# A retention, channel-mixing and gating kernel: the last two token blocks of the first channel mixing as a pair with seven products

## The chip, the cores and the metric

The kernel runs on one core of a Trainium2 chip. The metric is device time in microseconds (us) of one execution; several runs are taken and their median is given. The profile and the trace come from one further execution, whose own time is given beside its span.

Engines are named as in the profile: PE is TensorE's matmul, PEld its weight load, DVE is VectorE, ACT is ScalarE, POOL is GpSimd, SP is SyncE, which issues nearly all DMAs of this kernel in one queue.

## The reference

The reference computes three layers one after the other on 8 sequences of 576 tokens with 512 channels. The change lies in the second, in the first of its two channel products (`w_ch1`, 512 x 2048), and moves work of the second one (`w_ch2`).

```python
scores = scale * np.matmul(q, k.transpose(0, 1, 3, 2))      # retention, 8 heads of 64
attn = np.matmul(scores * Dmat, v)                          # Dmat: gamma ** (i - j), causal
xt = x.transpose(0, 2, 1)                                   # x: attn, heads joined
u = x + (xt @ U @ V).transpose(0, 2, 1)                     # low-rank token mixing, rank 32
ch = np.maximum(u @ w_ch1, 0.0) @ w_ch2                     # 512 -> 2048 -> 512
x = u + ch
k = np.maximum(xk @ w_k, 0.0)                               # xk, xr: x mixed with its neighbour
out = 1 / (1 + np.exp(-(xr @ w_r))) * ((k * k) @ w_v)
```

## The kernel before

The 4608 tokens are nine blocks of 512, numbered 0 to 8. A product in full precision is made of three matmuls: each operand is split into an upper part (a cast, on ACT) and a remainder (a subtraction, mostly on DVE), and upper x upper, lower x upper and upper x lower are summed in PSUM. All matmuls of the large products are 128x128 weights against 512 columns.

The order of all instructions is written out by hand: each engine runs its instructions in the order in which the code issues them, and SP's DMAs stand in one such order too. Tiles come from pools of slots (`big`, 35 slots of 4 KB a partition; `big2`, 16; `small`, 9 of 2 KB); a tile waits until its slot's last reader is done.

There are four stages.

1. **Retention** with the low-rank mixing, and beside it the first channel product. A step (`step_of`, L1307) does 128 tokens of one sequence; five steps make a sequence of 58 us. After the small matmuls of a step, `hidden` (L1058) issues some units of the first channel product out of the list `ready`. One unit (`hidden_part`, L360, three parts) gives 128 hidden features of one token block: 12 matmuls (L368), a relu on ACT (L374), a store to DRAM. 144 units in all: 9 blocks x 16 feature groups. `FULL` says how many follow each step of a sequence: 3, 3, 4, 4, 2. `todo` holds the mixing products of a finished sequence (`mix`, L1027), and at its end `mix_store` (L1033), which splits the mixed tokens into both blocks that the sequence touches, stores them, and puts 16 units in `ready`.
   When `todo` is empty, `slot` (L173) advances other jobs by a stage: they turn 64-bit weights into float32, split them and park them in DRAM (`park` L215 for `w_v`; `block_weight` L251 for `w_k` and `w_r`, with the four sums of blocks that a seven-product scheme needs).
2. **The rest of the first channel product**: when retention ends, 35 units are left (three of block 6 and the 32 of blocks 7 and 8), which run alone on PE. Beside them `second_weight` (L391) turns the eight groups of `w_ch2` into split block sums in SBUF; the last of them (`late`) works on DVE.
3. **The second channel product**, blocks 0 to 7 as four pairs with seven products instead of eight (`products`, L518): each item loads 1 MB of stored hidden values (`load_item` L464, four items ahead), forms sums (`sums_item` L476, two ahead, DVE), splits them (`split_item` L487, one ahead, ACT and DVE), and runs 24 or 18 matmuls (L540) into eight PSUM banks. Block 8 follows alone (`project`, L620 to L622).
4. **Gates, keys and values** of the third layer, the first two with seven products as well (`product`, L1411; its operands come from the generator `operands`, L679).

The pool of PSUM banks is handed over between stages 2 and 3 (`first_psum.close()`).

Of the kernel before, what the change touches and what calls it, by code (L numbers as in the profile page):

```python
# [30 lines left out]
L = 64  # L31
# [5 lines left out]
NF = DF1 // 128  # L37


@with_exitstack  # L40
def retention_mixer_kernel(ctx: ExitStack, tc: tile.TileContext, io):
# [142 lines left out]
    class Weight:  # L184
# [66 lines left out]
    def block_weight(g, pool, src, kept, kind):  # L251
        raw, a, got = [], [], {}

        def load():
            for i in range(2):
                r = pool.tile([128, 512], I64, tag="unit", name=f"w{kind}raw{g}_{i}")
                c0 = (g + len(kept) * i) * 128
                nc.sync.dma_start(
                    r.rearrange("p (k n) -> p k n", n=128),
                    src[:, c0:c0 + 128].rearrange("(k p) n -> p k n", p=128),  # L260
                )
                raw.append(r)
# [12 lines left out]
        def sums():  # L275
            x = got["s"] = [
                cv.tile([128, 512], F32, tag="cf", name="cf", bufs=5).rearrange(
                    "p (s n) -> p s n", n=256
                )
                for i in range(2)  # L280
            ]
            f = got["f"]
            a11, a12, a21, a22 = f[:, 0, :256], f[:, 0, 256:], f[:, 1, :256], f[:, 1, 256:]
            s1, s3, s2, s4 = (x[i // 2][:, i % 2] for i in range(4))
            nc.gpsimd.tensor_tensor(s1, a21, a22, op=ALU.add)
            nc.gpsimd.tensor_tensor(s2, s1, a11, op=ALU.subtract)
            nc.gpsimd.tensor_tensor(s3, a11, a21, op=ALU.subtract)
            nc.gpsimd.tensor_tensor(s4, a12, s2, op=ALU.subtract)

        def parts(i):  # L290
            h, l = (
                pool.tile([128, 4, 256], F32R, tag="unit", name=f"w{kind}{x}{g}_{i}") for x in "hl"
            )
            for w in range(2):
                if i == 0:
                    src = got["f"][:, w].rearrange("p (s n) -> p s n", n=256)
                else:
                    src = got["s"][w]
# [15 lines left out]
        ]  # L314

# [75 lines left out]
    def second_weight(j, pool):  # L391
        raw, got = [], {}
        out = pool if j else big2

        late = j == NF // 2 - 1

# [7 lines left out]
        def down():  # L404
            got["a"] = unit(big if late else big2, F32, f"w2a{j}")
            got["f"] = unit(big if late else big2, F32, f"w2f{j}")
            for i in range(2):
                high(got["a"][:, i], raw[i])
                low(got["f"][:, i].bitcast(U32), raw[i])
# [5 lines left out]
        def sums():  # L415
# [4 lines left out]
            eng = nc.vector if late else nc.gpsimd  # L420
# [24 lines left out]
        def parts_of_one(i):  # L445
            for lo in range(2):
                part(i, lo, nc.vector)

        return [
            load, *[None] * (5 if late else 1 if j else 2), down, lambda: fill(0), lambda: fill(1), sums,  # L450
            *(
                (lambda: parts_of_one(0), lambda: parts_of_one(1)) if late
                else (lambda: parts(0, nc.vector), lambda: parts(1, nc.gpsimd))
            ),
        ]
# [223 lines left out]
    def operands(x, q, a, b, nm):  # L679
        def upper(n, src):  # L680
            h, l = (unit(big, F32R, f"{nm}{y}{n}_{q}")[:, :, :columns(q)] for y in "hl")
# [8 lines left out]
        t = unit(big, F32, f"{nm}t_{q}")[:, :, :columns(q)]  # L690
# [5 lines left out]
        less(b[0], b[0], a[0])  # L696
        yield
        lower()
        lower = upper("t1", b[0])
        yield  # L700
        less(t, b[1], b[0])
# [49 lines left out]
    with ExitStack() as st:  # L751
# [280 lines left out]

        def mix_store(b):  # L1033
# [11 lines left out]
        todo, ready = [], []  # L1045

# [5 lines left out]
        def later(b):  # L1052
            for k in range(KD):
                for s in range(2):
                    todo.append(lambda k=k, s=s: mix(b, k, s))
            todo.append(lambda: mix_store(b))
# [110 lines left out]
        for at in (9, 10, 11, 13, 15, 17, 19):  # L1167
            waiting.insert(at, [None])
        for at, job in zip((0,4,8,12,16,20), jobs):
            waiting.insert(at, job)  # L1170

# [118 lines left out]
        FIRST, FULL = (2, 1, 2, 1, 1, 2, 2, 3), (3, 3, 4, 4, 2)  # L1290
# [15 lines left out]

        def step_of(i):  # L1307
# [8 lines left out]
            if p == NC - 1:  # L1316
                plan(i + 2, low_rank_sum, b)
                plan(i + 3, later, b)
            for fn, args in due.pop(i, []):
                fn(*args)  # L1320
            if not ready:
                mixes(9)
            n = FIRST[i - NC] if i < len(FIRST) + NC else FULL[p]
            for x in range(2):
                hidden((n + 1 - x) // 2, False)
                stages(2 * i + x)
                if i > 2 * NC + 2 and not todo:
                    quiet.append(i)
                    slot(new=len(quiet) % 2 == 1)
# [4 lines left out]
        for i in sorted(due):  # L1334
            for fn, args in due.pop(i):
                fn(*args)
            hidden(2)
        while todo:
            hidden(1) if ready else mixes(1)
        while waiting or going:  # L1340
            slot()

# [6 lines left out]
    for j in range(NF // 2):  # L1349
        waiting.append(second_weight(j, big))  # L1350
    ticks = []

    def tick():
        ticks.append(0)
        slot(new=len(ticks) in (27, 4 * (len(ticks) // 4) + 1) and len(ticks) < 28)

    while len(ready) > 2 * NF:
        hidden(1, False)
        tick()
    ready.sort(key=lambda x: x[1] + 2 * (x[0] == NB - 1))  # L1360
    while ready:
        if len(ready) in (7, 5, 3, 1):
            load_item(3 - len(ready) // 2)
        if len(ready) in (3, 1):
            sums_item(len(ready) == 1)
        if len(ready) == 2:
            split_item(0)
        hidden(1, False)
        tick()
    first_psum.close()  # L1370
    psum.append(ctx.enter_context(tc.tile_pool(name="psb", bufs=1, space=PSUM, reuse_waits="tile")))
    for n, (q, h, j) in enumerate(ITEMS):
# [4 lines left out]
        if n + 1 < len(ITEMS):  # L1377
# [5 lines left out]
        if n == len(ITEMS) - 1:  # L1383
            split_hidden(0)
        products(n)
# [286 lines left out]
```

## Time and profile before

| | us |
|---|---|
| median of 3 runs | 1353.21 (1351.12 to 1356.03) |
| the profiled execution's own time | 1349.82 |
| its span, first to last instruction | 1348.0 |
| PE busy, of the span | 1332.4 (99%) |
| DVE, ACT, POOL busy | 845.5, 652.1, 337.4 |
| TensorE's mean granted clock | 0.995 |
| moved by DMA | 308 MB, 229 GB/s |

A busy PE is a modelled time: matmuls overlap, and one of 512 columns is shown as up to 0.39 us long while the next starts sooner. What one costs in a row of them is read from the chain of work that ended last, where pieces of the same line are merged with their count. An idle time in brackets stands ahead of an instruction, with what ended it.

### The profile page before, as it was taken

The numbers are of one execution on the slowest core, as the hardware profiler recorded it, in microseconds if no ns is written. First come the engines' busy times: TensorE is split into PE (matmuls) and PEld (weight loads), VectorE is DVE, ScalarE is ACT, GpSimd is POOL, SyncE is SP. The second block draws the span as 40 slices with busy tenths as digits, with TensorE's granted clock in tenths as the row PEclk, the third lists the DMA queues.
The fourth block names the chain that finished last, engine by engine and source line by source line (L and its number), as shares of the span: only waits on it lengthen the run. The fifth ranks groups of instructions, "written<-read, shape, count | busy, mean of one in ns | idle before, by whom it ended". The sixth has DMA issues, their size and how long they took to land.

```text
span 1348.0 us, 25775 instructions
## 1 busy us (share of the span) xinstructions
PE 1332.4 (99%) x10263; PEld 1096.0 (81%) x10263; DVE 845.5 (63%) x1173; ACT 652.1 (48%) x1133; POOL 337.4 (25%) x284
## 2 busy tenths in 40 slices
PE   7999999999999999999999999999999999999998
PEld 4778888888887888888888888888888888888897
DVE  4763333243340223989897987897787787787753
ACT  4664444434343466544444434565464464464431
POOL 2121232412222154023222112204204204204212
PEclk8899999999999999999999999999999999999999
DMA  8977698776653657969697886794174174273372
GB/s 292 333 260 247 210 334 286 273 275 242 215 209 149 211 198 256 318 234 313 196 308 274 296 277 223 261 334 185 65 272 163 70 271 160 71 273 124 111 282 77
DMA packets 124377, 308.26 MB, mean 229 GB/s; under 512 B 14496, under 2 KB 27040, under 8 KB 124256
## 3 DMA queue, kind: packets, MB, share of 16 engines
q1 hardware_dynamic: 124256, 306.60, 65.5%
q8 instruction: 81, 1.33, 0.4%
q14 instruction: 40, 0.33, 0.1%
HBM read 215.33 MB, written 91.23 MB: 227 GB/s over the span
## 4 chain that ended last, share of the span: by engine, by line
PE 93%; DVE 4%; DMA 1%; issue 1%; ACT 1%; SPq 0%; POOL 0%; DVEq 0%; ACTq 0%
PE h L368 29%; PE v L1507 14%; PE ga L540 6%; PE gc L540 6%; PE gd L540 5%; PE kc L1411 4%; PE kd L1411 4%; PE ka L1411 4%; PE gb L540 3%; PE kb L1411 2%; PE rd L1411 2%; PE rc L1411 2%; PE ra L1411 2%; PE xn L962 2%; PE up L854 1%; PE dn L876 1%
## 5 line engine op out<-in xcount | busy, mean ns | idle before, releaser
L374 ACT ACTIVATE hs<-h 128x512 f32<-128x512 f32 x144 | 86.0, 598 | 211.8 <-PE h L368 208.2
L1463 POOL TENSOR_TENSOR vl<-m,vh 128x512 fp32r<-128x512 f32 (+1 forms) x40 | 47.6, 1191 | 310.3 <-ACT vh L1462 240.0
L834 DVE TENSOR_TENSOR pm<-up,dtab 128x512 f32<-128x512 f32 (+1 forms) x40 | 25.4, 636 | 134.1 <-PE up L820 121.6
L499 ACT CAST sbh<-rb 128x1024 fp32r<-128x1024 f32 x64 | 67.3, 1052 | 59.9 <-PE gd L540 43.4
L500 DVE TENSOR_TENSOR sbl<-rb,sbh 128x1024 fp32r<-128x1024 f32 x64 | 85.3, 1333 | 7.8 <-ACT sbh L499 7.7
L1507 PE MATMUL v<-vh,wv_0u 128*128 128x512 f32 x288 | 88.8, 389 | 0.0
L1507 PE MATMUL v<-vh,wv_1u 128*128 128x512 f32 x288 | 88.7, 389 | 0.0
L500 DVE TENSOR_TENSOR sal<-ra,sah 128x1024 fp32r<-128x1024 f32 (+1 forms) x64 | 65.5, 1023 | 20.6 <-PE gd L540 12.7
L499 ACT CAST sah<-ra 128x1024 fp32r<-128x1024 f32 (+1 forms) x64 | 53.6, 837 | 50.7 <-DVE ra L481 19.6
L782 POOL TENSOR_TENSOR kv<-kv,ktab 128x512 f32<-128x512 f32 (+1 forms) x40 | 39.8, 995 | 142.7 <-DMA kv<-in_kv 101.0
L1463 POOL TENSOR_TENSOR vl<-c,vh 128x512 fp32r<-128x512 f32 (+1 forms) x40 | 62.2, 1574 | 25.8 <-ACT vh L1462 25.8
L1507 PEld LDWEIGHTS v<-vh,wv_1u 128*128 128x128 f32 x288 | 54.1, 188 | 11.2
L1507 PEld LDWEIGHTS v<-vh,wv_0u 128*128 128x128 f32 x288 | 53.9, 188 | 11.0
L1462 ACT CAST vh<-m 128x512 fp32r<-128x512 f32 (+1 forms) x40 | 23.2, 579 | 75.7 <-DVE m L1461 75.7
L1031 DVE TENSOR_TENSOR xt<-mx,xt 128x256 f32<-128x256 f32 x64 | 28.8, 457 | 49.2 <-PE mx L1027 49.0
L1507 PE MATMUL v<-vl,wv_0u 128*128 128x512 f32 x144 | 56.0, 389 | 0.0
L1507 PE MATMUL v<-vl,wv_1u 128*128 128x512 f32 x144 | 56.0, 389 | 0.0
L653 ACT ACTIVATE tp<-x2l,omu 128x511 f32<-128x511 f32 x72 | 50.9, 712 | 2.7 <-DMA x2l<-xb 1.4
L584 POOL TENSOR_TENSOR x<-x,ur 128x512 f32<-128x512 f32 x16 | 24.3, 1530 | 107.5 <-DMA ur<-ub 53.5
L557 POOL TENSOR_TENSOR m<-m,ur 128x512 f32<-128x512 f32 x8 | 12.2, 1557 | 133.6 <-ACT m L554 133.6
L1461 DVE SCALAR_TENSOR_TENSOR m<-m 128x512 f32<-128x512 f32 (+1 forms) x40 | 44.8, 1120 | 1.4
L1411 PE MATMUL kc<-kht,wk 128*128 128x512 f32 (+1 forms) x160 | 45.5, 368 | 0.0
(290 smaller groups left out, 3740.3 us busy)
## 6 DMA issues: line engine op xcount, KB each, us to landing
wk<-keys SPq DMA_DIRECT2D x80, 512.0 KB, 6.0
hp<-hs SPq DMA_DIRECT2D x128, 256.0 KB, 2.9
rb<-hp SPq DMA_DIRECT2D x64, 512.0 KB, 5.8
wr<-gates SPq DMA_DIRECT2D x40, 512.0 KB, 6.9
qk<-in_qk SPq DMA_DIRECT2D x32, 512.0 KB, 5.6
kv<-in_kv SPq DMA_DIRECT2D x32, 512.0 KB, 6.2
ra<-hp SPq DMA_DIRECT2D x32, 512.0 KB, 7.1
ur<-ub SPq DMA_DIRECT2D x18, 512.0 KB, 5.8
```

The costliest lines, as they stand in the source:

```text
L368: nc.tensor.matmul(hps[t, f], w.part(lo, k, fo), u[k // 2][:, k % 2, :], start=(part == 0 and k == 0), stop=(part == 2 and k == KD - 1),)
L374: nc.scalar.activation(h, hps.pop((t, f)), AF.Relu)
L499: nc.scalar.copy(hi_, src)
L500: nc.vector.tensor_tensor(lo_, src, hi_.bitcast(F32), op=ALU.subtract)
L540: nc.tensor.matmul(group[g][p], l[:, col(p)], r, start=(h == 0 and j == 0 and i == 0), stop=(i == 2 and last), skip_group_check=True,)
L653: nc.scalar.activation(tp[:, 1:], x[:, :BT - 1], AF.Copy, scale=omu[:, j, k:k + 1])
L782: nc.gpsimd.tensor_tensor(k, k, ktab[:, p, :n].to_broadcast([128, n, NP, D]), op=ALU.mult)
L1031: nc.vector.tensor_tensor(u, ps[:, :n], u, op=ALU.add)
L1411: nc.tensor.matmul(ps[b], l, r[:, i], start=(part == 0 and i == 0 and j == 0), stop=(i == 1 and j == 2), skip_group_check=True,)
L1461: nc.vector.scalar_tensor_tensor(x, x, 0.0, x, op0=ALU.max, op1=ALU.mult)
L1463: eng.tensor_tensor(l, x, h.bitcast(F32), op=ALU.subtract)
L1507: nc.tensor.matmul(vacc[t][o], w.part(lo, g, col(o)), x[:, i, :], start=(g == 0 and i == 0 and j == 0), stop=(g == NG - 1 and i == 1 and j ...
```

## The change

Blocks 7 and 8 are taken out of the list of units and computed as a pair after retention, in eight groups (`first_group`) of seven products with six matmuls each. Their operands are seven sums and splits of the two blocks (`operands`, now with a pool argument, and writing into its first block instead of its second). The weights' sums are formed on DVE during retention out of the split weights (`first_sums`, one step in each `beside`), stored in DRAM, and loaded and split again a group ahead. The relu of these blocks works in SBUF, after the sums.

Four of the eight groups of `w_ch2` (`KEPT` = 4 to 7) are converted during retention by `block_weight` with a new argument `by_row`, parked, and loaded in the third stage (`load_second`); the other four are converted beside the new groups. The raw loads of `w_v` are issued two slots ahead of their conversion instead of one. Jobs begin in three of eight slots instead of every second. In sequences 2 to 6 the first part of a block is no longer split by the sequence before, but loaded again (`fetch_head`) and split (`split_head`) with its own sequence. The last sequence has 2, 2, 3, 3, 3 units after its steps. Cut to its core:

```diff
+HF = NF // 2
+PAIR = (NB - 2, NB - 1)
+KEPT = 4
-                waiting.append(convert(fetch, parts, 128, 512, store))
+                job = convert(fetch, parts, 128, 512, store)
+                waiting.append([job[0], None, *job[1:]])
+    def first_sums(g):      # stages: whole(0), whole(1), sums(0), sums(1), store
+        def whole(i):       # twice: 128x512 = upper part + remainder, on DVE
+            f = g + HF * i
+            for k in range(2):
+                nc.vector.tensor_tensor(
+                    got["x"][:, 2 * i + k].rearrange("p (k n) -> p k n", n=128),
+                    w.h[k][:, :, c].bitcast(F32), w.l[k][:, :, c].bitcast(F32), op=ALU.add)
+        def sums(i):        # two of 128x256 each
...
+    def load_first(g):
+        fraw[g] = (big if g < 2 else big2).tile([128, 4, 256], F32, tag="unit", name=f"fr{g}")
+        nc.sync.dma_start(fraw[g], kept_1[g])
+
+    def split_first(g):
+        x = fraw.pop(g)
+        fs[g] = h, l = tuple(
+            (big2 if g else big).tile([128, 4, 256], F32R, tag="unit", name=f"f{y}{g}") for y in "hl")
+        nc.scalar.copy(h, x)
+        nc.vector.tensor_tensor(l, x, h.bitcast(F32), op=ALU.subtract)
+    def load_second(j, i):  # two loads of 512 KB
...
-            load, *[None] * (5 if late else 1 if j else 2), down, lambda: fill(0), ...
+            load, None, lambda: words(0), lambda: words(1), lambda: fill(0), lambda: fill(1), sums,
+            lambda: parts(0, nc.vector), lambda: parts(1, nc.gpsimd),
         def mix_store(b):
-            split_u(b, BT - o, u[:, :, :o], o)
-            split_u(b + 1, 0, u[:, :, o:], S - o)
+            if b < PAIR[0]:
+                split_u(b, BT - o, u[:, :, :o], o)
+            if b == 0:
+                split_u(1, 0, u[:, :, o:], S - o)
-            ready.extend((b, f) for f in range(NF))
-            if b == B - 1:
-                ready.extend((b + 1, f) for f in range(NF))
+            if b < PAIR[0]:
+                ready.extend((b, f) for f in range(NF))
...
+        def beside():
+            quiet.append(0)
+            slot(new=len(quiet) % 8 in (1, 4, 6))
+            if sums and len(quiet) > 8:
+                sums.pop(0)()
+            n = ... FULL[p] if b < B - 1 else LAST[p]          # LAST: 2, 2, 3, 3, 3
...
+        gen = operands(x1, 0, even, odd, "f")
+        next(gen)
+        while ready:                                           # units left of block 6
+            if len(ready) in (4, 3):
+                load_first(4 - len(ready))
+            if len(ready) == 1:
+                split_first(0)
+            t, f = ready.pop(0)
+            for part in range(3):
+                hidden_part(t, f, part)
+                next(gen, None)
+        slot(new=len(ticks) % 6 == 1)                          # in tick()
+    def first_group(g, base, extra):
+        ps = {nm: bank(base + i, f"f{nm}{g}") for i, nm in enumerate("abcd")}
+        for m, (b, new, w, nm) in {1: ("a", ...), 7: ("c", ...), 5: ("d", ...), 2: ("b", ...),
+                                   6: ("a", ...), 4: ("c", ...), 3: ("d", ...)}.items():
+            xh, xl = x1[0, nm]
+            for i in range(2):
+                for j, (lo, x) in enumerate(((0, xh), (1, xh), (0, xl))):
+                    nc.tensor.matmul(ps[b], w(lo, i), x[:, i], ...)
+            if m in (1, 7, 6):
+                kept[m] = small(F32, f"f{m}_{g}")
+                nc.scalar.copy(kept[m], ps[b])
+            elif m == 5:
+                nc.vector.tensor_tensor(kept[7], ps[b], kept[7], op=ALU.add)
+                while exits:
+                    exits.pop(0)()                             # last sum and relu of group g - 1
+            elif m == 2:
+                nc.vector.tensor_tensor(kept[1], ps[b], kept[1], op=ALU.add)
+                out(PAIR[0], g, kept[1])                       # relu on ACT, store
+            else:
+                nc.vector.tensor_tensor(x, ps[b], kept[6], op=ALU.add)
+                out(PAIR[m == 3], g + HF * (m == 4), x)
+            for fn in extra.get(m, ()):
+                fn()
+            if m in (1, 5, 6, 3):
+                tick()
+    for g in range(HF):
+        if g + 1 < HF:
+            extra[7] = [lambda g=g: split_first(g + 1)]
+        if g + 2 < HF:
+            extra[2] = [lambda g=g: load_first(g + 2)]
+        if g == HF - 2:
+            extra[5] = [lambda: load_item(0)]
+            extra[4] = [lambda: load_item(1)]
+        if g == HF - 1:
+            extra[1] = [lambda: load_item(2), lambda: sums_item(0)]
+            extra[7] = [lambda: split_item(0)]
+            extra[5] = [lambda: load_item(3), lambda: sums_item(1)]
+            extra[6] = [lambda: split_item(1)]
+        first_group(g, 4 * (g % 2), extra)
     for n, (q, h, j) in enumerate(ITEMS):
-        if n + 1 < len(ITEMS):
+        if 0 < n < len(ITEMS) - 1:
             split_item(n + 1)
+        if n < HF - KEPT:
+            load_second(KEPT + n, 0)
+        elif n >= HF - 2 and n - HF + 2 < HF - KEPT:
+            load_second(KEPT + n - HF + 2, 1)
```

## Rows read from the trace of the kernel before

**Rows 1.** The page's parts 1 and 4: busy time, and the chain's shares.
```profile
PE 1332.4 (99%) x10263; PEld 1096.0 (81%) x10263; DVE 845.5 (63%) x1173; ACT 652.1 (48%) x1133; POOL 337.4 (25%) x284
...
PE 93%; DVE 4%; DMA 1%; issue 1%; ACT 1%; SPq 0%; POOL 0%; DVEq 0%; ACTq 0%
```

**Rows 2.** The chain in order of time: start us, us, what; matmuls in unbroken series.
```profile
441.40 94.80 PE h L368 x418
...
544.78 1.37 PE gc L540 x6
...
888.64 2.72 PE ra L1411 x12
```

**Rows 3.** Busy time by stretch of time; the first line names the columns.
```profile
core 0: us, PE busy (x) PEld busy (x) DVE busy (x) ACT busy (x) POOL busy (x), PEclk, DMA share, GB/s
...
343.00:402.00 59.00, 59.00 (x814) 48.09 (x815) 19.49 (x38) 21.86 (x41) 12.85 (x13) 1.00 0.61 212
402.00:441.00 39.00, 39.00 (x227) 31.25 (x226) 5.87 (x13) 13.04 (x25) 9.25 (x9) 1.00 0.40 149
441.00:537.00 96.00, 96.00 (x426) 79.50 (x425) 25.38 (x37) 55.72 (x100) 38.37 (x42) 1.00 0.67 226
...
541.00:563.00 22.00, 21.85 (x97) 17.77 (x96) 21.72 (x30) 12.89 (x15) 0.00 (x0) 1.00 0.96 345
```

**Rows 4.** The timeline at 154 us and at the first items: start, us, what.
```profile
154.66 0.19 PEld L1027 LDWEIGHTS mx<-vst,gt 96*128 96x128 f32 x1 [0.56 <-issue]
...
543.58 0.19 PEld L540 LDWEIGHTS ga<-sal,w2p 128*128 128x128 f32 x1 [0.57 <-DVE sal L500]
...
546.05 0.69 DVE L480 TENSOR_TENSOR rb<-rb,ra 128x512 f32<-128x512 f32 x1
```

**Rows 5.** The chain just ahead of that wait at 154 us.
```profile
149.00 3.79 DMA wv_raw<-in_moe_w_v
```

**Rows 6.** Groups by line and shape: the durations that answer to the added work.
```profile
L1491 DVE TENSOR_TENSOR m<-m,m 128x512 f32<-128x512 f32 x16 | 28.5, 1784 | 0.0
L684 DVE TENSOR_TENSOR kl<-x2l,kh 128x1024 fp32r<-128x1024 f32 x12 | 14.7, 1221 | 3.7 <-ACT kh L683 3.7
L1446 DVE TENSOR_TENSOR r<-r,r 128x512 f32<-128x512 f32 x8 | 5.5, 684 | 0.0
L580 DVE TENSOR_TENSOR x<-gc,u 128x512 f32<-128x512 f32 x8 | 5.5, 692 | 9.6 <-PE gc L540 9.6
L923 DVE TENSOR_TENSOR w<-dn,w 128x256 f32<-128x256 f32 x56 | 23.5, 420 | 5.5 <-ACT w L921 4.6
L374 ACT ACTIVATE hs<-h 128x512 f32<-128x512 f32 x144 | 86.0, 598 | 211.8 <-PE h L368 208.2 <-issue 3.3
L499 ACT CAST sbh<-rb 128x1024 fp32r<-128x1024 f32 x64 | 67.3, 1052 | 59.9 <-PE gd L540 43.4 <-DMA rb<-hp 5.6 <-PE ga L540 3.3
L1477 ACT COPY m<-ka 128x512 f32<-128x512 f32 x32 | 18.5, 577 | 1.1 <-PE ka L1411 1.1
L97 ACT ACTIVATE w2a<-w2raw 128x512 f32<-128x512 f32 x16 | 10.6, 664 | 0.0
L438 ACT CAST w2q<-w2f 128x512 fp32r<-128x512 f32 x8 | 5.0, 622 | 0.0
L439 POOL TENSOR_TENSOR w2q<-w2s,w2q 128x512 fp32r<-128x512 f32 x7 | 9.5, 1356 | 0.0
L421 POOL TENSOR_TENSOR w2s<-w2f 128x256 f32<-128x256 f32 x7 | 5.1, 734 | 26.5 <-DVE w2f L104 26.5
```

**Rows 7.** DMA issues of the whole run: count, KB each, median us to landing.
```profile
rb<-hp SPq DMA_DIRECT2D x64, 512.0 KB, 5.8
...
x2l<-xb SPq DMA_DIRECT2D x18, 512.0 KB, 8.9
...
wv_1u<-wv_kept SPq DMA_DIRECT2D x4, 512.0 KB, 9.9
```

**Rows 8.** Weight loads by line and shape, of the units.
```profile
L368 PEld LDWEIGHTS h<-ul,w_0h 128*128 128x128 f32 x144 | 27.0, 188 | 5.7
```

More of the change, by code (lines that the diff above doesn't have):

```diff
@@ L404, in down, with words @@
         def down():
[L405 to L409, printed above, removed]
+            got["a"] = unit(big2, F32, f"w2a{j}")
+            got["f"] = unit(big2, F32, f"w2f{j}")
+        def words(i):
+            if i == 0:
+                down()
+            high(got["a"][:, i], raw[i])
+            low(got["f"][:, i].bitcast(U32), raw[i])
         def fill(i):
@@ L443, in parts @@
                 part(i, lo, eng)
-        def parts_of_one(i):
-            for lo in range(2):
-                part(i, lo, nc.vector)
         return [
[L450 to L454, printed above, removed]
-        ]
+            load, None, lambda: words(0), lambda: words(1), lambda: fill(0), lambda: fill(1), sums,
+            lambda: parts(0, nc.vector), lambda: parts(1, nc.gpsimd),
+        ]
+    def load_second(j, i):
+        w = (wp, wq)[i]
+        w[j] = []
+        for lo in range(2):
+            x = big.tile([128, 4, 256], F32R, tag="unit", name=f"w2{'pq'[i]}{j}_{lo}")
+            nc.sync.dma_start(x.bitcast(F32), kept_2[j][:, i, lo])
+            w[j].append(x)
     def col(p):
@@ L677, in mixed, with operands @@
                 yield
-    def operands(x, q, a, b, nm):
+    def operands(x, q, a, b, nm, where=None):
+        where = where or big
         def upper(n, src):
-            h, l = (unit(big, F32R, f"{nm}{y}{n}_{q}")[:, :, :columns(q)] for y in "hl")
+            h, l = (unit(where, F32R, f"{nm}{y}{n}_{q}")[:, :, :columns(q)] for y in "hl")
             x[q, n] = h, l
@@ L689, in operands @@
         lower = upper("11", a[0])
-        t = unit(big, F32, f"{nm}t_{q}")[:, :, :columns(q)]
+        t = unit(where, F32, f"{nm}t_{q}")[:, :, :columns(q)]
         less(t, b[1], b[0])
@@ L695, in operands @@
         yield
-        less(b[0], b[0], a[0])
+        less(a[0], b[0], a[0])
         yield
         lower()
-        lower = upper("t1", b[0])
+        lower = upper("t1", a[0])
         yield
-        less(t, b[1], b[0])
+        less(t, b[1], a[0])
         yield
@@ L1166, in retention_mixer_kernel @@
         jobs += [block_weight(g, big, io["moe2_w_r"], kept_r, "r") for g in range(2)]
-        for at in (9, 10, 11, 13, 15, 17, 19):
-            waiting.insert(at, [None])
-        for at, job in zip((0,4,8,12,16,20), jobs):
+        jobs += [block_weight(j, big, io["moe_w_ch2"], kept_2, "s", True) for j in range(KEPT, HF)]
+        for at, job in zip((0, 1, 2, 4, 5, 6, 8, 10, 12, 14), jobs):
             waiting.insert(at, job)
+        sums = []
+        for g in range(HF):
+            x = first_sums(g)
+            if sums:
+                before, begin = sums[-1], x[0]
+                sums[-1] = lambda before=before, begin=begin: (before(), begin())
+                x = x[1:]
+            sums.extend(x)
         def load_to(n):
@@ L1327, in step_of @@
                 if i > 2 * NC + 2 and not todo:
-                    quiet.append(i)
-                    slot(new=len(quiet) % 2 == 1)
+                    beside()
         first_batch()
@@ L1336, in retention_mixer_kernel @@
                 fn(*args)
-            hidden(2)
+            hidden(1)
+            beside()
+            hidden(1)
+            beside()
         while todo:
             hidden(1) if ready else mixes(1)
+            beside()
         while waiting or going:
             slot()
+        assert not sums
+        x1 = {}
+        gen = operands(x1, 0, even, odd, "f")
[9 more added lines that the diff above has]
+                next(gen, None)
+        for _ in gen:
+            pass
     big2 = ctx.enter_context(tc.tile_pool(name="big2", bufs=16, reuse_waits="tile"))
@@ new lines, in retention_mixer_kernel @@
+    for g in range(HF):
+        extra = {}
+        if g + 1 < HF:
[11 more added lines that the diff above has]
+        first_group(g, 4 * (g % 2), extra)
@@ L1372, in retention_mixer_kernel @@
+    while exits:
+        exits.pop(0)()
     for n, (q, h, j) in enumerate(ITEMS):
```

132 lines of the change are left out of this document (101 added, 31 removed).

## The prediction

> **What bounds the kernel now.** I read the page's shares first: PE is busy for 99% of the span, and 93% of the chain that ended last is PE [rows 1]. A busy PE can still be a slow one, so the chain in order of time comes next. It shows what a product costs when nothing holds it up: 418 matmuls of the units in 94.80 us, 0.2268 us each; six of the second channel product in 1.36 to 1.37 us, 0.227; twelve of the third layer in 2.72, 0.227 [rows 2]. Every 512-column matmul of the kernel runs at this pace. Between 45 us and the end I find only a few us in which PE waits, most of it where an item of a new pair meets banks that are not yet free. Two of those waits lie in the change's way: 0.57 us at 543.58 on DVE, and 0.56 us at 154.66 [rows 4], behind a wait of ScalarE for a raw load of `w_v` [rows 5]. Last I read the busy times by stretch, to see what the other engines have to spare [rows 3]: in retention (343 to 402) DVE 19.5, ACT 21.9 and POOL 12.9 of 59 us; while the units run alone (441 to 537) DVE 25.4, ACT 55.7, POOL 38.4 of 96; but in the first four items (541 to 563) DVE is full, 21.72 of 22 us, and the DMA engines are at 0.96, 345 GB/s.
>
> So a matmul less is time won if what stands beside it keeps up.
>
> **What is removed.** Blocks 7 and 8 took 2 x 16 units of 12 matmuls, 384. The pair takes 8 groups x 7 products x 6, 336. 48 matmuls x 0.2268 [rows 2] = **10.9 us**. Nothing else on PE changes in number. Before, 35 units stood after retention (420 matmuls, the 94.80 us and a few more); after, I count 6 units and the 336, 408 in all; the other 36 matmuls (three units, 8.2 us) go from the last sequence, where `LAST` sums to 13 instead of 16.
>
> **Retention carries more (0 to +1 us; I take 0).** DVE forms the weights' sums: per group four 128x512 additions at 0.684 and four 128x256 ones at 0.420 [rows 6], 4.4 us, 35 us for eight. The four parked groups of `w_ch2` add per group to ACT four conversions at 0.664 and four casts at 0.622, 5.1 us; to POOL four sums at 0.734 and four remainders at 1.356, 8.4 us [rows 6]; 20 and 33 us in all. This is spread over some 270 us where DVE is idle for 40 of 59 us and POOL for 46 [rows 3]. A stage of a job stands behind the step's own DVE work, and the next of that is needed only after at least two units, 5.4 us; my count of stages in one step never comes above 5.1 us on ACT or 4.1 on DVE, spread over its two halves. Without that cover the price would be the excess of single steps; the wait at 154 us shows the size, half a us. SP's queue gets stores and reloads, each issued a stage after what it waits for. The 0.56 us at 154 us goes, since the load has two slots: -0.3 (the rest of that gap is the matmul's own pace).
>
> **Into the groups (0 to +2.3; I take 0.2).** The operands need seven casts at 1.05, and seven remainders and four differences at 1.22 [rows 6], 13.4 us of DVE, beside six units, 16.3 us of PE. That fits. But by my count `big` holds 16 tiles of `w_ch1`, 4 of block 6, up to 14 of operands and 4 of weight sums, more than 35, so the last of them wait for block 6's last unit. If that is the first split of weight sums, cast and remainder, 2.3 us, follow the unit, and only 1.36 us of product 1 covers them; block 6's upper parts come free 0.9 us earlier, though, which leaves about nothing.
>
> **In a group (0 to +1 in each; 0.4 in all).** Seven products last 9.52 us. ACT has three copies at 0.577, four relus at 0.598 and a cast at 1.05, 5.2 us, and 2.6 for the four jobs that run beside eight groups (5.1 each); DVE four additions at 0.69, one at 0.68 and a remainder at 1.22, 4.7 us. Both fit. What could stop PE is order: product 5's addition stands on DVE behind the remainder of the next group's weight sums, which stands behind its cast on ACT, and product 3 needs that bank 4.08 us after product 5 ends, at 8.16 us. Usually: copy until 3.3, cast 4.4, remainder 5.6, addition 6.3. Where two jobs overlap (one's two casts beside the next's two conversions, 2.6 us), it is about 8.1: two groups without slack, for which I take 0.2 each.
>
> **Out of the groups (0 to +7.6; I take +2.1).** Here is the one new wait that I expect. In the last group DVE also forms and splits items 0 and 1, and the additions that free its last two banks (products 4 and 3) stand behind item 1's remainders. Item 0's product 5 wants these banks third, 9.52 + 4.08 = 13.6 us after the group began. DVE, from item 0's landing at about 2.0 (its 1 MB is asked for some 4 us before the group begins and takes 5.8, [rows 7]): two sums at 0.69 [rows 4] to 3.4; ACT's cast to 4.4; two remainders 6.9; product 5's addition, the last group's sum, item 1's sums, product 2's addition 10.3; then ACT's relu, copy and cast, 2.2, to 12.5; two remainders 15.0; product 4's addition 15.7. So 15.7 - 13.6 = 2.1 us. Without a wait for load or ACT it would be done at 11.8, and the price 0. If POOL slows the five SBUF sums as in the row at 1.784 us [rows 6], 5 x 1.1 more: 7.6. The old wait of 0.57 us at 543.58 goes with the old order, some 0.4 of it beyond the pace.
>
> **Items (0 to +5.6; I take 0).** The last conversion's DVE work leaves the full stretch. But `load_second` puts 1 MB into each of the first four items: 1 + 0.25 + 1 MB in 5.44 us, 434 GB/s, against 345 in that stretch [rows 3]. At 345 each item's transfers take 6.8 us, 1.4 too long, 5.6 after four. An item's load is asked for at least two items, 10.9 us, ahead of its sums and needs 5.8 [rows 7], so 5.1 of it is hidden.
>
> **Sum.** -10.9 - 0.3 - 0.4 + 0.2 + 0.4 + 2.1 = -8.9. The profiled execution, 1349.82 us, becomes about 1340.9. It was 3.4 us under the median of the runs (1353.21), which I put down to the spread between executions (1351.12 to 1356.03): the forecast for the median is **1344.3**.
>
> A page would size the first term otherwise. The Trainium skill (TensorE: Matmul & The Clock Gate, Back-to-back issue gap) gives a sustained 131 ns for a matmul of 512 columns in a stream of weight loads and matmuls; by it the 48 would be worth 6.3 us. This trace shows 226.8 in the longest unbroken series, so the row decides.
>
> **Rivals.**
> - *No new wait*: the join costs nothing, the groups run like the old units: 1353.2 - 11.6 = 1341.6. For it: every wait that I found is one of order, and small shifts remove it.
> - *The joins bite*: DVE's sums are stretched by POOL, each group loses up to a us (8 us, since POOL's remainders and sums fall into most groups), or the exit costs its upper bound, 7.6 instead of 2.1: about 1350 to 1352. For it the row at 1.784 us; against it that DVE's remainders beside POOL in the items keep a mean near 1.3.
> - *The weights' sums land late (slower)*: a group's sums are asked for behind product 2's relu and store, up to 7.6 us into the group before, and ACT waits for them in order, with product 5's addition behind it. That leaves 9.5 - 7.6 + 8.2 - 3.0 = 7.1 us for the landing. At the 9.9 us that a load of this size took in the third layer [rows 7] six groups would lose 2.8 each, 16.8 us: 1361. It turns slower than before from about 8.6 us of landing. Against it: `rb` lands in 5.8 with the DMA engines nearly full.
> - *The products don't run at the pace of the units*, so that their number saves less. The page's 131 ns is that case, with 6.3 us instead of 10.9: 1348.9. The weight loads, 188 ns [rows 8], are shorter than the pace, and the new matmuls have the shape of the old.
>
> **How the numbers follow.** Forecast 1344.3, its own range 1342 to 1347.5: 0.64. No new wait 0.14, the joins 0.12, late sums 0.07, pace 0.03. A range of 8 in 10 takes in the first two and the joins' lower part, and the spread of a median: 1339.8 to 1350.5. About 0.3%, 4 us, is what a measurement of this kernel can tell from no change. Faster by more: the forecast, no new wait, most of pace, a little of the joins, 0.83; within: 0.11; slower: 0.06.
>
> **What would show it.** The pair's products as unbroken series of 1.36 us, 336 of them; a wait of PE of about 2 us on an addition of DVE at the first item's product 5; none at 154 us; no PE wait for casts of weight sums in the groups. Wrong would be: a wait in each group, a retention sequence longer than 58 us, or raw loads and stores that push the items' loads past 11 us.

## The result, and the profile after

The changed kernel takes 1367.16 us (median of 4 runs, 1365.13 to 1368.03), the kernel before 1352.52 beside it: a ratio of 1.0102 (95% interval 1.0079 to 1.0125). It is 1% slower; the forecast was 1344.3, with 1350.5 as the upper end. The profiled execution took 1365.13 us with a span of 1363.0, 15.0 us more than the span before.

The page after, part 1, and one line of part 4 (its chain was followed back over 59% of the span only, so the waits are read by stretch instead); they answer to [rows 1]:

```profile
PE 1330.8 (98%) x10215; PEld 1090.4 (80%) x10215; DVE 934.2 (69%) x1276; ACT 676.0 (50%) x1166; POOL 359.7 (26%) x300
...
PE 58%; DVE 1%; issue 0%; ACT 0%; DVEq 0%
```

48 matmuls are gone, as counted, and DVE is busy for 89 us more. To see where the 15.0 us come from, I subtracted the starts of the same matmuls in the two traces, stage by stage:

| stage, after minus before | predicted | measured |
|---|---|---|
| up to 153 us | 0 | +0.7 |
| the wait at 154 us | -0.3 | -0.35 |
| retention, 168 to 376 us | 0 | **+7.0** |
| 48 matmuls | -10.9 | -10.9 |
| the last six units, into the groups | +0.2 | +1.1 |
| the eight groups (9.52 us each without waits) | +0.4 | **+14.1** |
| items, join among them | +2.1 - 0.4 | +3.4 |
| everything behind them | 0 | 0.0 |

So the saving came whole, and two stages that I had priced at almost nothing took twice of it. Busy time in these two, after (the columns are those of [rows 3]):

```profile
168.00:376.00 208.00, 203.29 (x2743) 165.26 (x2741) 119.92 (x199) 97.56 (x184) 96.45 (x89) 0.99 0.95 332
...
458.70:549.00 90.30, 80.43 (x337) 63.50 (x337) 47.49 (x67) 54.95 (x93) 21.64 (x24) 0.98 0.58 194
```

and the first of them before, where PE had no gap at all:

```profile
168.00:376.00 208.00, 208.00 (x2892) 169.96 (x2891) 67.76 (x130) 86.55 (x162) 65.24 (x63) 1.00 0.78 272
```

No engine is full in either stage: in the groups DVE is busy for 47 of 90 us and ACT for 55. What stops PE there is order, as the experiments show. **The groups**: the waits of PE, then of ACT, then of DVE, from 458 to 556 us (engine, line, what released it: us in total, times, longest):

```profile
PE fd L1512 <- DVE f L1520: 5.1, 5, 2.2
PE fa L1512 <- ACT f L1518: 2.8, 2, 2.5
PE fc L1512 <- ACT f L1518: 1.9, 2, 1.5
PE gd L599 <- DVE f L1528: 1.9, 1, 1.9
```

```profile
ACT f L1493 <- DVE f L1536: 17.7, 7, 2.7
ACT f L1493 <- DVE f L1524: 7.9, 6, 2.6
...
DVE fl L371 <- ACT fh L370: 23.9, 7, 5.2
```

L1518 is the copy out of a bank, L1520 product 5's addition, L1524 product 2's, L1536 the group's last sum, L1493 a relu, L370 and L371 cast and remainder of the next group's weight sums. ACT waits for DVE and DVE for ACT, turn by turn. The timeline of both from 494.88 us on shows one such round (start, us; in brackets the idle time before and its releaser):

```profile
494.88 1.05 ACT L370 CAST fh<-fr 128x1024 fp32r<-128x1024 f32 x1 [0.63 <-DMA fr<-first]
495.96 1.32 DVE L371 TENSOR_TENSOR fl<-fr,fh 128x1024 fp32r<-128x1024 f32 x1 [2.79 <-ACT fh L370]
497.20 0.68 DVE L1520 TENSOR_TENSOR f<-fd,f 128x512 f32<-128x512 f32 x1
497.80 0.68 DVE L1536 TENSOR_TENSOR f<-f,f 128x512 f32<-128x512 f32 x1
498.51 0.64 ACT L1493 ACTIVATE f<-f 128x512 f32<-128x512 f32 x1 [2.59 <-DVE f L1536]
499.05 0.60 ACT L496 CAST w2p<-w2f 128x512 fp32r<-128x512 f32 x1
...
499.69 0.69 DVE L497 TENSOR_TENSOR w2p<-w2f,w2p 128x512 fp32r<-128x512 f32 x1 [1.21 <-ACT w2p L496]
...
500.90 0.69 DVE L1524 TENSOR_TENSOR f<-fb,f 128x512 f32<-128x512 f32 x1
501.62 0.63 ACT L1493 ACTIVATE f<-f 128x512 f32<-128x512 f32 x1 [1.44 <-DVE f L1524]
502.16 0.57 ACT L1518 COPY f<-fa 128x512 f32<-128x512 f32 x1
502.62 0.62 ACT L496 CAST w2p<-w2s 128x512 fp32r<-128x512 f32 x1
```

Read it as one rope: cast, remainder, addition, sum, relu, two casts of a `w_ch2` job, two remainders, addition, relu, and only then the copy of product 6, whose last matmul started at 496.00. ACT then does a job's casts and conversions and two relus, and copies the next group's product 1 at 506.93; PE has waited for that:

```profile
506.93 0.58 ACT L1518 COPY f<-fa 128x512 f32<-128x512 f32 x1
...
507.55 0.50 PE L1512 MATMUL fa<-fht,fh 128*128 128x512 f32 x1 [2.50 <-ACT f L1518]
```

A PE gap is then paid a second time. In the 3.7 us of this gap PE is busy for 1.20; in the stretch behind it the granted clock is 0.51, the lower of the two levels:

```profile
505.00:508.70 3.70, 1.20 (x6) 0.97 (x6) 1.41 (x1) 3.70 (x7) 0.86 (x1) 1.00 0.54 208
508.70:512.10 3.40, 3.40 (x10) 2.64 (x9) 3.13 (x5) 0.87 (x2) 0.02 (x1) 0.51 0.02 5
```

In those 3.4 us eight matmuls start, 0.427 us apart, in place of 15 (0.2268 each): 1.6 of the groups' 14.1 us, with about as much again in retention behind 276 to 280 us, and at the first items.

**Retention**: the 7.0 us lie at two places, 2.0 at 211 to 219 us and 5.0 at 263 to 283. The timeline of DVE at the second, and of PE at the end of the same delay:

```profile
271.18 1.59 DVE L340 TENSOR_TENSOR fs<-w_1h,w_1l 128x256 f32<-128x256 f32 x2 [7.14 <-DMA gates<-wrh]
...
273.30 2.25 DVE L340 TENSOR_TENSOR fs<-w_3h,w_3l 128x256 f32<-128x256 f32 x2
275.47 0.68 DVE L895 TENSOR_TENSOR pm<-up,dtab 128x512 f32<-128x512 f32 x1
...
278.52 0.41 PE L1088 MATMUL mx<-vst,gt 96*128 96x320 f32 x1 [2.42 <-DVE xt L1092]
```

The first addition of a new `fs` tile waits 7.14 us, not for its data but for a slot of `big` whose last reader is a store of gate weights. The step's own mask (`pm`) stands behind it on DVE, and so do 3.8 us of the sums' additions; these rows alone don't say which of the two made it late. ACT has such a wait for a slot at 211 us:

```profile
211.04 0.68 ACT L104 ACTIVATE wrf<-wrraw 128x512 uint32<-128x512 uint8 x1 [2.63 <-DMA keys<-wkh]
```

Two expected sights are there too. The wait at 154 us [rows 4] is down to 0.24 (PEld):

```profile
155.06 0.19 PEld L1088 LDWEIGHTS mx<-vst,gt 96*128 96x128 f32 x1 [0.24 <-issue]
```

and the reload of weight sums, the rival that I feared, lands in 3.7 us (`rb` in 6.7, [rows 7]):

```profile
rb<-hp SPq DMA_DIRECT2D x64, 512.0 KB, 6.7
...
fr<-first SPq DMA_DIRECT2D x8, 512.0 KB, 3.7
```

### The profile page after: what moved, and what is told of

It reads as the page before. It is cut to its first block, busy times and chain, and to the rows that moved or that the text cites. A ratio compares the mean times of both kernels' runs of the same rounds, so it can differ in the third digit from the quotient of the medians.

```text
span 1363.0 us, 26017 instructions
## 1 busy us (share of the span) xinstructions
PE 1330.8 (98%) x10215; PEld 1090.4 (80%) x10215; DVE 934.2 (69%) x1276; ACT 676.0 (50%) x1166; POOL 359.7 (26%) x300
## 4 chain that ended last, share of the span: by engine, by line
PE 58%; DVE 1%; issue 0%; ACT 0%; DVEq 0%
PE v L1697 14%; PE gd L599 6%; PE ga L599 6%; PE gc L599 6%; PE kd L1601 4%; PE kc L1601 4%; PE ka L1601 4%; PE gb L599 3%; PE kb L1601 2%; PE rd L1601 2%; PE rc L1601 2%; PE ra L1601 2%; PE c L681 1%; PE c L679 1%; PE c L680 1%; PE rb L1601 1%
## 5 line engine op out<-in xcount | busy, mean ns | idle before, releaser
L431 ACT ACTIVATE hs<-h 128x512 f32<-128x512 f32 x112 | 67.0, 598 | 172.5 <-PE h L425 164.1
```

The source lines that it names most:

```text
L431: nc.scalar.activation(h, hps.pop((t, f)), AF.Relu)
```

## The experiments

All changes are to the changed kernel. "Retention" is the loss from 168 to 376 us against before (units that `LAST` moves taken out), "groups" the time from the first to the last group's end (76.2 without waits), "items" that of the 64 items (307.6 before). Times of single executions differ by several us among themselves (the kernel before: 1349.2 to 1356.8), and the first 168 us alone by up to 5.6, so they are read by stage. Times with one decimal are of a single run, and every stage is of one execution. The stages vary too: six executions with the same code in retention (changed, e1, e2, e4, e7, e9) lose 3.4 to 8.8 us there.

| kernel | us | retention | groups | items |
|---|---|---|---|---|
| changed | 1367.16 | +7.0 | 90.3 | 310.9 |
| e1_no_conversions | 1417.0 | +7.0 | 78.4 | 373.9 |
| e2_split_after | 1359.7 | +3.4 | 84.8 | 311.7 |
| e3_three_steps_ahead | 1401.7 | +28.9 | 90.7 | 311.1 |
| e5_no_sums | 1363.8 | +0.7 | 91.7 | 310.9 |
| e4_join_after | 1367.4 | +7.9 | 89.9 | 311.7 |
| e6_own_tile | 1378.7 | +9.3 | 89.2 | 311.6 |
| e7_spread | 1368.9 | +8.1 | 88.8 | 310.8 |
| b1_all_mended | 1368.67 | +11.9 | 77.4 | 311.2 |
| e9_order_in_groups | 1355.2 | +8.8 | 76.2 | 310.8 |
| e10_two_tiles | 1363.6 | +5.2 | 89.5 | 311.5 |
| b3_mended_two_tiles | 1353.92 | +4.0 | 77.4 | 311.1 |
| b5_sums_later | 1351.07 | +1.9 | 76.2 | 310.6 |
| b6_rest_slower | 1351.36 | +3.7 | 76.2 | 313.1 |

### What holds the groups up

**e1_no_conversions** loads parked groups where the first four groups of `w_ch2` were converted.

```diff
-    for j in range(KEPT):
-        waiting.append(second_weight(j, big))
...
+        if g > 3:
+            extra[6] = [lambda g=g: load_second(g - 4, 0)]
...
```

> Leaves out the conversion of the first four groups of w_ch2 beside the new groups: the four parked groups are loaded in their place too (so the second product uses wrong weights for half of its groups). In the changed kernel the eight groups take 90.3 us from the first group's start to the first item's, where 336 matmuls at 0.2268 would take 76.2; groups 0 and 1 take 9.52 us, groups 2, 4 and 5 take 11.65, 13.94 and 12.79. Theory (ScalarE runs in order, and the conversions with their raw loads stand ahead of the copies and of the cast that product 5's addition waits for): groups at 76.5 to 78.5 us, all of 9.5 to 9.8, no stretch at half clock in them. Rival (the weight sums' own load and split, or the relu's stores, hold the groups up): 86 us or more.

Seven groups took 9.52 us, the last 2.2 more. Without the conversions in ACT's queue the groups lose nearly nothing. (All `w_ch2` tiles then lie in `big`, and the items wait for slots: the time as a whole says nothing.)

**e2_split_after** moves cast and remainder of the next group's sums from product 7 to product 2.

```diff
-            extra[7] = [lambda g=g: split_first(g + 1)]
+            extra[2] = [lambda g=g: split_first(g + 1)]
```

> The split of the next group's weight sums is issued after product 2's addition instead of after product 7's copy, so that product 5's addition doesn't stand behind it on VectorE; nothing else. Theory that the order behind the split is most of the loss (waits of PE on product 5's addition: 5.1 us of 9.8 us of waits in the groups): 90.3 becomes 80 to 84 us, and what is left are waits for copies of products 1 and 7. Rival (ScalarE is simply full where two conversions overlap): 87 us or more, the waits only change their name.

5.6 us less, and the wait moves: in four groups product 7 now waits for the split itself (`fc <- DVE fl`, 3.1 us in all, and `fc <- ACT fh`, 0.9). That lies between the two expectations: one link of the rope is cut, the rest holds.

**e7_spread** gives each conversion its own stage, one behind every product.

```diff
...
-            if m in (1, 5, 6, 3):
-                tick()
+            tick()
```

> The same conversions of the first four groups of w_ch2, in stages of one ScalarE operation each, one stage behind each of the seven products, a new job every 12 products. Theory (what the groups lose is the time that a copy out of a bank stands behind several conversions in ScalarE's queue): the groups shrink from 90.3 us to 79 to 84 us, and the time by as much, to 1355 to 1361 us. Rival (ScalarE has too much to do in the groups in all, however it is ordered): the groups keep 87 us or more.

A miss: 88.8 us. The bunching alone is not the cause.

**e9_order_in_groups** leaves the conversions as they are and changes only the order: a relu is issued one product after its addition, the cast at product 5, the remainder behind product 2's addition.

```diff
-            nc.scalar.activation(x, x, AF.Relu)
+            relus.append(lambda: relu(t, f, x))
...
-            extra[7] = [lambda g=g: split_first(g + 1)]
+            extra[5] = [lambda g=g, rests=rests: rests.append(split_first(g + 1))]
+            extra[2] = [lambda rests=rests: rests.pop()()]
...
```

> The conversions stay bunched as in the changed kernel; only the order in the groups is changed: each relu is issued one product later than its addition, and the next group's sums are split with the cast at product 5 and the remainder behind product 2's addition. Theory A (the two queues wait for each other: a copy behind a relu behind an addition behind a remainder behind a cast): the groups shrink from 90.3 us to 77 to 80 us, as they did to 77.4 with everything mended. Theory B (the bunches of conversions ahead of the copies are a second cause by themselves): 82 to 87 us, since spreading them alone gave 88.8.

Every group takes 9.52 us. Its busy times over all groups:

```profile
463.30:539.40 76.10, 76.10 (x337) 63.04 (x336) 48.05 (x68) 55.90 (x94) 23.45 (x24) 1.00 0.71 235
```

DVE and ACT work as much as in the changed kernel (48 and 56 us) and PE never waits: theory A, and a little better than its range. e1 is no contradiction: the loss needs both, the conversions as time in each turn of the rope and the order that ties them to PE. Which of e9's two changes does more was not tested apart.

### The join at the first items

**e4_join_after** puts item 1's sums and splits behind product 3's addition.

```diff
-            extra[5] = [lambda: load_item(3), lambda: sums_item(1)]
-            extra[6] = [lambda: split_item(1)]
+            extra[5] = [lambda: load_item(3)]
+            extra[3] = [lambda: sums_item(1), lambda: split_item(1)]
```

> In the last group the sums and splits for item 1 stand behind product 3's addition instead of among products 5 and 6. My theory (order of the joins on VectorE): the 2.0 us that PE waits at item 0's product 5 goes to 0.5 or less and the rest of the kernel keeps its times, so some 2 us less than the changed kernel, with the groups' 90 us as they are. Rival (VectorE and ScalarE are simply behind by that much at the end of the groups): the wait moves to another product of items 0 or 1 and the sum of the gaps there stays near 2 us.

The wait at product 5 is gone, and the items take 311.7 us, not less than 310.9. Neither expectation holds as written: items 0 and 1 lose 0.1 us between them, and the waits stand at items 3, 4, 10 and later, on the splits of the items:

```profile
PE ga L599 <- DVE sal L559: 3.6, 5, 1.5
...
PE gc L599 <- DVE sbl L559: 0.5, 1, 0.5
```

In the changed kernel all of the 3.4 us are lost in the first two items. Where that wait is shorter or gone, later items lose about as much: in e9, whose groups lose nothing, the items still take 310.8. The trace of b5_sums_later (below), in which the first two items lose nothing, shows where it goes. DVE's waits for loads in the first 44 us of its items, of which the kernel before has none:

```profile
DVE rb L543 <- DMA rb<-hp: 9.0, 4, 2.7
DVE ra L547 <- DMA rb<-hp: 2.1, 1, 2.1
```

and the second half of these 44 us, in b5_sums_later and then in the kernel before (columns of [rows 3]):

```profile
552.49:574.49 22.00, 21.91 (x93) 16.82 (x93) 15.64 (x19) 10.35 (x14) 0.33 (x1) 1.00 1.03 412
```

```profile
559.38:581.38 22.00, 22.00 (x99) 18.22 (x98) 16.45 (x20) 10.14 (x15) 3.93 (x3) 1.00 0.74 245
```

The loads of `load_second` now stand between those of the items. From item 4 to item 8 the loads `rb` land 5.7 to 5.9 us apart, an item lasts 5.44 us, and DVE forms the sums of one item before it splits the item ahead of it, so each late load holds back a split. DVE ends the split `sal` of item 8 only 2.6 us before PE needs it, in the kernel before 6.5. Then POOL begins the finishing additions, beside which DVE's operations take 1.7 to 1.8 us instead of 0.7, in both kernels. They use up the lead: b5_sums_later loses 1.3 us up to item 8 and 2.1 more up to item 12, 3.4 in all, the kernel before 0.4. This is read from the traces; no run leaves out these loads alone.

### What holds retention up

**e3_three_steps_ahead** loads a step's keys and values one step later, to leave slots free.

```diff
-            load_to(i + 4)
+            load_to(i + 3)
```

> Retention's inputs are loaded three steps ahead instead of four, which leaves two more slots of the pool big free; the work is the same. In the changed kernel the sequences from 168 us to 376 us fall 7.0 us behind the kernel before, with VectorE and ScalarE waiting for slots whose last reader is a store (7.1 us behind gates<-wrl, 2.8 and 2.6 behind keys). Theory (slots): the loss falls to 0 to 2 us. Rival (the engines have too much work in some steps): it stays at 5 to 7. If the inputs come too late instead, PE waits on kv.

It took away the lead that the loads need: PE waits up to 2.1 us for `kv` and up to 3.2 for `qk` in several steps, and some 9 us are lost before the sums even begin. It tells nothing of the question.

**e5_no_sums** leaves out the sums of `w_ch1` (parked key weights are loaded in their place).

```diff
...
-            x = first_sums(g)
-            if sums:
+            x = []
+            if sums and x:
```

> Leaves out the forming of the weights' sums in retention (the groups load parked weights of the keys in their place, so blocks 7 and 8 come out wrong): 35 us of VectorE, one slot of big and 4 MB of stores less. Theory (slots): some of the 7.0 us stays, since the jobs' own pieces still wait for slots (ScalarE's wait of 2.6 us at 211 us): 1 to 4 us. Rival (VectorE's work): all of it goes. The groups are as in the changed kernel, 90 us.

The loss goes, with all of the parked conversions still there:

```profile
168.00:376.00 208.00, 207.46 (x2844) 169.07 (x2843) 76.79 (x139) 102.52 (x193) 93.88 (x90) 1.00 0.92 322
```

So the sums cause it, with 43 us more of DVE (119.92 - 76.79). All of it going is what the rival said, but the edit takes away the buffers together with the work, so which of them it is stays open here.

**e6_own_tile** gives the sums one tile for all groups (and no longer joins a group's first stage to the store of the group before).

```diff
-            if not i:
-                got["x"] = big.tile([128, 4, 256], F32, tag="unit", name=f"fs{g}")
+            if not got:
+                got["x"] = big.tile([128, 4, 256], F32, tag="unit", name="fs")
...
```

> The eight sums of w_ch1 share one tile for all groups, taken once, instead of a new buffer of the pool for each; VectorE's work and the stores stay. Theory (in the retention stage the wait of VectorE for a pool buffer that a store still reads, is what delays the chain): the loss from 168 us to 376 us against the kernel before falls from 7.0 us (3.4 in one other run) to 0 to 2, and the time to 1360 to 1364 us. Rival (VectorE's added work itself is what delays): the loss stays at 3.4 to 7.0 us and the time at 1364 to 1368 us.

My edit did the opposite of what I meant: each group now waits for its own tile's store of one stage before. DVE's wait from 168 to 430 us:

```profile
DVE fs L341 <- DMA first<-fs: 64.7, 7, 16.2
```

The loss grows to 9.3 us, hardly more than the 8.8 that the unchanged code can lose, but 9.9 us more are lost in the last sequence, where the other versions with the unchanged code lose at most 0.3. The same operations with more waiting for a buffer cost more: that speaks for the buffers.

**e10_two_tiles** uses two tiles in turn.

```diff
...
+                if g % 2 not in tiles:
+                    tiles[g % 2] = big.tile([128, 4, 256], F32, tag="unit", name=f"fs{g % 2}")
+                got["x"] = tiles[g % 2]
```

> The sums of w_ch1 use two tiles of their own in turn, so that a group's first operation waits only for the store of the group before the last (four stages, some 20 us, earlier) and for no store of another job. Theory (VectorE's wait for a buffer that a store still reads is what delays the chain; with one tile it waited 64.7 us and the kernel lost 12 us more): VectorE waits 0 to 2 us for stores, the loss between 168 and 376 us is 0 to 2 us, and the time 1358 to 1363 us. Rival (the added operations themselves delay it): loss of 3.4 us or more, 1364 us or more.

DVE waits for a store once, 2.9 us at 187 us, where it costs nothing; the wait at 271 us is gone. At that place 1.8 us are lost now and 0.4 in b3, which has the same tiles (5.0 in the changed kernel, 1.5 to 6.2 in the five other executions of its code), with the same additions on DVE. But 5.2 us are still lost in all, 3.3 of it at 212 to 219 us, behind a wait of ACT:

```profile
ACT wrf L104 <- DMA keys<-wkl: 4.2, 1, 4.2
```

That is a slot again, of another job and on another engine. My theory of DVE's wait alone falls short.

**b5_sums_later** has e9's order, e4's join, e10's tiles, and begins the sums twelve slots later.

```diff
...
-            if sums and len(quiet) > 8:
+            if sums and len(quiet) > 20:
```

> Groups with the changed order alone (conversions bunched, as in the changed kernel), item 1's joins behind the last product, two tiles for the sums, and the sums begun twelve slots later (behind the 20th quiet slot in place of the 8th). Theory: the 3.6 us that the version with two tiles still loses at 212 to 219 us are one wait of ScalarE for a pool buffer (4.3 us for a store of keys) at the time when the sums take theirs; begun later they lose 0 to 1 us, the groups stay at 76 to 77.5 us, and the time is 1348 to 1352 us. Rival (the sums lose it wherever they begin): a loss of 3 to 4 us again, at their new place, and 1352 to 1355 us.

Retention loses 1.9 us, above the 0 to 1 expected, though some two thirds of the sums' work still lie in this stretch (DVE 104.8 us, against 76.8 without any sums):

```profile
168.00:376.00 208.00, 206.34 (x2929) 168.54 (x2924) 104.83 (x181) 100.32 (x189) 98.08 (x92) 1.00 0.95 332
```

Together with e10 and b3 that points mainly to slots of `big`: an engine that takes one while a store still reads it stands, with its queue. Not every such wait costs: here DVE stands 4.7 us at 268 us for a store, and PE waits nowhere behind it. What share DVE's work has, the runs don't tell. In its 10 runs the kernel takes 1351.07 us, 0.9981 (0.9962 to 0.9999) of before: about 2 us faster, as is b6 below (0.9986, 0.9973 to 0.9999), by intervals that end just short of 1.

### All together

**b1_all_mended** joins e9's order, e7's stages, e4's join and e6's tile.

> The spread conversions, the joins of item 1 behind the last product, the sums in their own tile, each relu issued one product later than its addition, and the split of the next group's sums with its cast at product 5 and its remainder behind product 2's addition. Theory: groups of 76.5 to 79.5 us, no wait over 0.5 us at the first item, a retention loss of 0 to 2 us, so 1346 to 1352 us in all: the pair then gains 1 to 6 us on the kernel before. Rival (the pair's vector work costs what its matmuls save, wherever it is put): 1354 us or more.

The groups are mended (77.4), and e6's tile gives it all back in retention: 1.0108 (1.0077 to 1.0138).

**b3_mended_two_tiles** has e10's tiles instead.

> The kernel with everything mended, with two tiles for the sums in place of one. Theory: its groups stay at 77 to 78 us, its retention loses 0 to 2 us against the kernel before in place of 12 and more, and the last sequence's 10 us are not lost: 1346 to 1351 us, 1 to 6 us faster than the kernel before. Rival (the retention stage has no room for the sums): 1354 us or more.

1.0011 (0.9999 to 1.0023): no difference from before. The retention loss of 4.0 us is twice what I allowed, at 212 to 219 us; b5 was made for that.

**b6_rest_slower** is b5 with the items' finishing additions spread out.

```diff
-        for _ in range(2):
+        for _ in range(2 if j in (5, 6) else 1):
```

> As the kernel with the sums later, and the items' finishing steps (GpSimd's and VectorE's additions of products 1 to 7) issued one an item in place of two, two at the sixth and seventh. Theory (in the items VectorE's two-input operations take 1.77 us in place of 0.68 beside GpSimd's, and the split for the next item is late by it): the waits of over 0.5 us at items 8 to 11 go, the items take 308 to 309.5 us in place of 310.8 to 311.1, and the time is 1 to 2 us less than without it. Rival (the lateness is of the weights' parking and loads): no change, within 0.5 us.

The time, 1351.36, is that of b5 within 0.5 us, as the rival said. In the profiled execution the items take 313.1 us, longer, with five waits on `sal` in place of three. So spreading the finishing steps doesn't help: their lateness begins with the loads, as read above. In retention its code is b5's, yet it lost 3.7: 2.8 of it before 282 us, behind 7.2 us in which a new `fs` tile waited for a slot that POOL still read. Which slot a tile meets differs between executions.

## Why the prediction was wrong

- **What is removed**: right. 336 matmuls in 76.16 us (e9), 0.2267 each; everything behind the items is unchanged. The Trainium skill (TensorE: Matmul & The Clock Gate, Back-to-back issue gap) gives a sustained 131 ns for a matmul of 512 columns; these runs do not show it.
- **In a group, +0.4**: the step that failed, by 13.7 us. I summed each engine's work, 7.8 us on ACT and 4.7 on DVE of 9.52, saw that product 5's addition stands behind a cast, and let the queue start empty in every group. But ACT's queue carries over: relus wait for DVE's additions, those for a remainder, that for the cast, and a job's casts and conversions stand between. My own worst case (8.1 of 8.16 us) should have been carried into the next group instead of being priced at 0.2; the rival "the joins bite" had 8 us for it, for another reason, and too little.
- **Retention, 0**: the second failure, 7.0 us. I priced the sums as work (35 us; measured 43, of DVE's 119.9 against 76.8 without them) and found room for it. All eight additions of a group are 128x256, not four of them 128x512 as I wrote, so alone they would be 27 us (64 at 0.42); by their own rows they are busy for 49.5, since half of them fall beside POOL. The Trainium skill (GPSIMD Engine Reference, 1. Specifications) names contention between POOL and a DVE instruction with two SBUF inputs. The trace agrees: 30 additions that run beside POOL for most of their time take 0.83 to 1.52 us, the 34 others 0.41 to 0.43. But the size is not the main failure: I counted the slots of `big` for the groups and not for retention, where the sums' tile and a tile of ACT's wait behind stores.
- **The wait at 154 us, -0.3**: right, -0.35.
- **Into the groups, +0.2**: 1.1, of it 0.65 on one late relu of a unit.
- **Out of the groups, +2.1**: the wait stood where I put it, at product 5, at 1.9 to 2.0 us. The agreement is luck: I summed it for a last group of 9.52 us, and it took 12.6. In e9, where it does take 9.52 with item 1's joins in the same place, the wait is 0.9. Nor is it a price: without it (e4) the items lose as much elsewhere. With the low clock behind that wait the items cost 3.4.
- **Items, 0**: the third failure, hidden in the changed kernel by the wait ahead of it. I saw that `load_second` asks for 434 GB/s, and let 5.1 us of lead hide it. But that lead was needed later, for the finishing additions beside POOL: in b5_sums_later it is down to 2.6 us at item 8, and some 3 us are lost by item 12.
- **Weights' sums land late**: did not happen; ACT waits for `fr` 1.6 us in all, since it lands in 3.7.

What would have shown it from the trace of before: nothing there waits like this, so the only way was to write the two queues out over two groups in turn, with each instruction's partner, not their sums.

## What to carry to other kernels

Where two in-order engines hand work back and forth, the sum of each engine's work says nothing; follow the order over two rounds, and issue an operation that waits for the other engine only behind those that don't (relus one product later, and a split taken apart, mended 14 us). A tile taken from a full pool can cost what the slot's last reader still needs, and where that is a store, everything queued behind the taker waits too; count slots where a tile is taken, not where it is used. A lead that hides late loads is spent by them: see what needs it next. A wait that vanishes under an edit is a gain only if the stage gets shorter.

## What was unexpected of the hardware

In the changed kernel two long gaps of PE were followed by 3.4 us at the lower level of the granted clock (0.51), which costs about 1.6 us more: behind 276 to 280 us (PE busy for 1.57 of 4.0) and behind 505 to 508.7 (1.20 of 3.7). It doesn't always follow: in b6_rest_slower a gap of the same 2.42 us (PE busy for 1.58 of 4.0, from 278 to 282 us) left the clock at 1.00. And one and the same addition of DVE takes 0.69 us or 1.78, by what POOL does; in the items of b5_sums_later, POOL had been idle for 51 us until 574.16:

```profile
571.22 0.69 DVE L547 TENSOR_TENSOR ra<-rb,ra 128x512 f32<-128x512 f32 x1
...
574.16 3.07 POOL L620 TENSOR_TENSOR m<-m,ur 128x512 f32<-128x512 f32 x2 [51.14 <-ACT m L617]
574.29 1.78 DVE L547 TENSOR_TENSOR ra<-rb,ra 128x512 f32<-128x512 f32 x1
```
